# Seven block products for eight in the V and Q projections of a gated linear-attention and Mish kernel

## The chip, the cores and the metric

The kernel runs on one core of a Trainium2 chip. A core has five engines with instruction queues of their own: TensorE (PE, matrix products; PEld is its weight load), VectorE (DVE), ScalarE (ACT), GpSimd (POOL) and SyncE (SP, which here only issues DMAs). An engine takes its instructions in order; semaphores make one wait for another. The metric is the device time of one execution in microseconds (us), the median of several runs. Lower is better.

## What is computed

With S = 2048 rows, width D = 512, 32 heads of 16 columns, and a hidden width of 1376:

```python
g = sigmoid((x * gate_w).sum(-1, keepdims=True))
q, k, v = split(x @ wqkv)                       # each S x 512, 32 heads of 16
pq, pk = per head: q @ w_phi, k @ w_phi
phi = concat(softmax(p), softmax(-p))           # 32 features a head, for pq and for pk
kv, z = phi_k^T v, sum over rows of phi_k       # over all 2048 rows
a = (phi_q kv / (phi_q z + 1e-6)) @ wo
b = mish(x @ w1 + b1) @ w2
return g * a + (1 - g) * b
```

## The kernel before

Every product in fp32r is made of three: each operand is split into a high part (a copy to fp32r, on ACT) and a low part (the rest, a subtraction), and high x high, high x low and low x high are added in PSUM. `w_phi` is multiplied into the weights of K and Q at the start ("fuse").

**Phase A** runs over eight row chunks c = 0..7 of 256 rows, two tiles t of 128 rows each. PE computes K, V and Q of both tiles, each 12 matmuls of 128x128 by 128x512 (`proj`: four k tiles, three products each). For K the features follow: `mx`, `mn`, `d0`, `d1` on DVE (row maxima and differences, from PSUM), `E` on ACT (exp), `S`, `rS`, `ml` on DVE (sum, reciprocal, multiply). `z` on POOL adds E to `zacc`, an SBUF tile. V is copied from PSUM by ACT (`ve`); Q is copied (`qe`) and stored to a DRAM buffer `pqd` (`st`). The product of E and V, `kv`, is 64 small matmuls a chunk into one PSUM bank, issued for several chunks at once. Meanwhile ACT (`xh`) and POOL (`xl`) split the next chunk's x, and `wh`, `wl` split the weights w1 and w2 of phase B, a piece of 1024 columns at a time, all 44 KB a partition of w2 in phase A.

At the end of phase A, `zt zf zs zl` reduce `zacc` over partitions and broadcast it back (`zb`); `km` masks kv.

**Phase B** runs over four blocks of 512 rows. For the hidden slices i = 0..10 of 128 columns PE computes `up` (12 matmuls), ACT the Mish (`mi`) and the high part (`hi`), POOL the low part (`lo`), and PE `dn` (12 matmuls, four row tiles, accumulated over i in four PSUM banks). In between, for each of four row tiles, the features of Q are computed on DVE and ACT (`lq mx mn d0 d1 E S T rS D m de rd sc es tr`), stored to DRAM and read back in another order (`ed`, then `mv` into `eT`), multiplied by kv (`nu`), split (`oh` on ACT, `ol` on DVE), multiplied by wo (`wo`), and joined with the dense branch (`ag`, `fi`), which also stores the output. `XH`, `XL` split x for the next block.

The order is written out by hand: strings of step names (`FIRST`, `MID`, `BLOCK0` and so on) are run one by one, each step appends its instructions to its engine's queue, and `keep_in_program_order` keeps them so. A suffix names another chunk or block: `'` the one before, `"` the one before that, `+` the next. So a step's place in the string fixes its place in each engine's queue, SP's too, where a DMA that waits holds up all behind it. Tiles come from pools with a fixed number of buffers a tag; an allocation waits until an earlier tile of the tag is free. In PSUM, tag `a` has three banks, `dn` four and `kv` one.

Of the kernel before, what the change touches and what calls it, by code (L numbers as in the profile page):

```python
# [32 lines left out]
WARM = 10  # L33

# [11 lines left out]
THREE = MID + """ kv" kv' kv """  # L46
SIXTH = """
    k0 xh mx0 mn0 d00 d10 xl ldx k1 wh0 E0 wl0 ldw0 mx1 mn1 d01 d11 v0 wh1 E1 S0 rS0 ml0 z0 ve0 v1 wl1 ldw1 lq0+
    S1 rS1 ml1 z1 ve1 q0 qe0 st0 q1 qe1 st1 mx0+ mn0+ kv" kv' kv
"""  # L50
NEXT = """
    lq1+ d00+ d10+ k0 xh mx0 mn0 d00 d10 xl ldx k1 wh0 E0 wl0 ldw0 E0+ mx1 mn1 d01 d11 wh1 E1 S0 rS0 ml0 z0 v0 ve0 wl1 ldw1
    S1 rS1 ml1 z1 v1 ve1 q0 mx1+ mn1+ d01+ d11+ qe0 st0 q1 qe1 st1 E1+
"""
LAST = """
    lq2+ k0 mx0 mn0 d00 d10 k1 ldw0 E0 XH0 mx1 mn1 d01 d11 wx E1 v0 S0 rS0 ml0 z0 ve0 XH1 S1 rS1 ml1 z1 XL0
    v1 ve1 mx2+ mn2+ XL1 q0 qe0 st0 q1 qe1 st1 zt zf zs S0+ zl kv' kv rS0+ km
"""

BLOCK0 = """
    up0 lq3 mi0 gr hi0 lo0 ldo0 ldo1 S1 rS1 up1 up2 mi1 hi1 lo1 wh0 wl0 d02 d12 T0 D0 m0 de0 rd0 sc0 es0 tr0 mi2 hi2 up3 dn0 hc lo2
    mi3 hi3 lo3 T1 D1 m1 de1 rd1 sc1 es1 tr1 mv0 lq0+ lq1+ mx3 mn3 d03 d13 WH0 dn1
    up4 mi4 hi4 lo4 WH1 WL0 dn2 E2 S2 T2 rS2 D2 m2 de2 rd2 sc2 es2 tr2 up5 mi5 hi5 lo5 WL1 dn3 E3 ge gg up6 mi6 hi6 lo6 dn4
    up7 mi7 hi7 lo7 dn5 S3 T3 rS3 D3 m3 de3 rd3 sc3 es3 tr3 mv1 up8 mi8 hi8 lo8 dn6
    mx0+ mn0+ d00+ d10+ mx1+ mn1+ d01+ d11+ lq2+ lq3+ up9 mi9 hi9 lo9 dn7 E0+ E1+ S0+ T0+ LX0 rS0+ D0+ m0+ de0+ rd0+ sc0+
    up10 mi10 hi10 lo10 dn8 dn9 cd nu0 nu1 oh0 ol0 es0+ tr0+ XH0+ XL0+ S1+ T1+ rS1+ LX1 df0 df1 wo0 ag0 wo1 oh1 ol1 ag1 D1+ fi0
    m1+ de1+ rd1+ sc1+ df2 df3 wo2 ag2 fi1 XH1+ XL1+ es1+ fi2 wo3 ag3 fi3 tr1+ mv0+
"""  # L70
BLOCK1 = """
    up0 mi0 hi0 lo0 gr mx2 mn2 d02 d12 mx3 mn3 d03 d13 up1 mi1 hi1 lo1 lq0+ lq1+ E2 E3 hc S2 T2 rS2 D2 m2 de2 rd2 sc2 es2 tr2
    up2 mi2 hi2 lo2 dn0 S3 T3 rS3 D3 m3 de3 rd3 sc3 es3 tr3 mv1 up3 mi3 hi3 lo3 dn1 up4 mi4 hi4 lo4 dn2
    mx0+ mn0+ d00+ d10+ mx1+ mn1+ d01+ d11+ lq2+ lq3+ up5 mi5 hi5 lo5 dn3 E0+ E1+ ge gg
    S0+ T0+ rS0+ D0+ m0+ de0+ rd0+ sc0+ es0+ tr0+ up6 mi6 hi6 lo6 dn4 up7 mi7 hi7 lo7 dn5 cd nu0 nu1 oh0 ol0 S1+ T1+ rS1+ D1+ LX0 LX1
    m1+ de1+ rd1+ sc1+ es1+ dn6 wo0 ag0 wo1 ag1 oh1 ol1 tr1+ mv0+ dn7 up8 mi8 hi8 lo8 mx2+ mn2+ d02+ d12+ mx3+ mn3+ d03+ d13+
    wo2 ag2 up9 mi9 hi9 lo9 dn8 E2+ E3+ up10 mi10 hi10 lo10 wo3 ag3 XH0+ XL0+ XH1+ XL1+ dn9 df0 fi0 df1 fi1 df2 fi2 df3 fi3
"""
BLOCK = """
    up0 mi0 hi0 lo0 gr lq0+ lq1+ S2 T2 rS2 D2 m2 de2 rd2 sc2 es2 tr2 up1 mi1 hi1 lo1 hc up2 mi2 hi2 lo2 dn0  # L80
    S3 T3 rS3 D3 m3 de3 rd3 sc3 es3 tr3 mv1 up3 mi3 hi3 lo3 dn1 up4 mi4 hi4 lo4 dn2
    mx0+ mn0+ d00+ d10+ mx1+ mn1+ d01+ d11+ lq2+ lq3+ up5 mi5 hi5 lo5 dn3 E0+ E1+ ge gg
    S0+ T0+ rS0+ D0+ m0+ de0+ rd0+ sc0+ up6 mi6 hi6 lo6 dn4 cd nu0 nu1 oh0 ol0 es0+ tr0+ S1+ T1+ rS1+ D1+ LX0 LX1 m1+ de1+ rd1+ sc1+
    es1+ dn5 wo0 ag0 wo1 ag1 oh1 ol1 tr1+ mv0+ dn6 up7 mi7 hi7 lo7 wo2 ag2 mx2+ mn2+ d02+ d12+ mx3+ mn3+ d03+ d13+
    up8 mi8 hi8 lo8 dn7 E2+ E3+ up9 mi9 hi9 lo9 wo3 ag3 up10 mi10 hi10 lo10 dn8 XH0+ XL0+ XH1+ XL1+ dn9 df0 fi0 df1 fi1 df2 fi2 df3 fi3
"""
# [3 lines left out]
def tile_gated_mix(ctx: ExitStack, tc: tile.TileContext, xT, wv, wkT, wqT, bd, w1a, w1b, b1, w2a, w2b, wo, out):  # L90
# [159 lines left out]
    def feat_ops(key, t, src, d):  # L250
# [7 lines left out]
        def dd(a):  # L258
            if "E" not in d:
                pair = key, t // 2  # L260
                if key == ("A", NCH - 1):
                    d["E"] = k4("E", "oh")
                else:
                    if pair not in Ep:
                        e = T([P, NFB * 512], F32, "w2b", 2, "E")[:, :2048] if key in THIRD else k8("E", "E", F32)[:, :]
                        Ep[pair] = e.rearrange("p (t x) -> p t x", t=2)
                    d["E"] = Ep[pair][:, t % 2, :]
            E = hv(d["E"][:, a * 512 : (a + 1) * 512])
            if a == 0:
                pin(V.tensor_sub(E, hv(src()), d["mx"][:, :, None].to_broadcast([P, H, DH])))  # L270
            else:
                pin(V.tensor_sub(E, d["mn"][:, :, None].to_broadcast([P, H, DH]), hv(src())))  # L272
# [15 lines left out]

    def a_ops(c):
        key = ("A", c)  # L290
        P_ = psA[c] = {}
        for t in range(2):
# [37 lines left out]
            at(key, f"z{t}", lambda d=d: pin(G_.tensor_add(zacc, zacc, d["E"])))  # L330
# [14 lines left out]
        at(key, "kv", kv)  # L345
        if c + 1 < NCH:
# [48 lines left out]
    def w2_tile(f, x):  # L395
        n_, f = ("w2a", f) if f < NFA else ("w2b", f - NFA)
        return W[n_][0][x][:, f * 512 : (f + 1) * 512]

    w2x = {}

    def w2_ops(key):
        def wx():
            h, l = w2_tile(NFA - 1, 0), w2_tile(NFA - 1, 1)
            w2x.update(a=h, b=const.tile([P, 512], F32R, name="w2x"), c=l)
            for dst, o, src, i, n in (("b", 0, h, 0, GROW), ("a", GROW, l, 32, 32), ("b", GROW, l, 0, 32)) + tuple(("c", o, l, 64, 32) for o in (0, 32, 96)):
                pin(Sy.dma_start(f32(w2x[dst][o : o + n, :]), f32(src[i : i + n, :])))

        at(key, "wx", wx)  # L410

# [100 lines left out]
    def b_ops(b):  # L512
# [83 lines left out]
        at(key, "gr", gr)  # L596
        at(key, "ge", ge)
# [294 lines left out]
```

## Time and profile before

| | |
|---|---|
| runs | 444.24, 444.59, 444.80 us; median 444.59 us |
| span of the profiled execution, first to last instruction | 442.5 us; median of the runs less this span: 2.1 us |
| PE / DVE / ACT / POOL busy | 437.8 / 313.2 / 201.4 / 159.6 us |
| DMA | 49.64 MB, mean 112 GB/s |

The profile is of one execution. It comes without a whole time of its own beside the span; so the span, plus the 2.1 us by which the median of the runs exceeds it, stands for that execution's time below. Busy time is the union of an engine's instructions. A chain of waits follows the work back from the last instruction. A row of a group gives line, engine, operation, output<-input, shapes and count, then total busy us and mean ns, then the idle time ahead of them and what ended it. A row of a timeline gives start and duration in us.

### The profile page before, as it was taken

To read this page: it belongs to the slowest core of one execution; us is meant where nothing else is said; L and a number is where in the kernel's file an instruction comes from. 1 tells how busy PE (TensorE), PEld (TensorE's weight loads), DVE (VectorE), ACT (ScalarE), POOL (GpSimd) and SP (SyncE) were. 2 spreads that over 40 slices of the span, in tenths; PEclk is the share of its full clock that TensorE was granted. 3 is DMA by queue.
4 is the path that set the end of the run, shared out by engine and by line. 5 is a ranking of instruction groups with operands and counts; after the bars stand their busy time and mean duration, and the time that the engine had idled before them with its cause. 6 is when DMAs were issued, how large, how long until landed. Compare 5 with 4: busy or idle time off the path is not lost.

```text
span 442.5 us, 7179 instructions
## 1 busy us (share of the span) xinstructions
PE 437.8 (99%) x2874; PEld 359.9 (81%) x2874; DVE 313.2 (71%) x420; ACT 201.4 (46%) x286; POOL 159.6 (36%) x100
## 2 busy tenths in 40 slices
PE   8999999999999999999999999999999999999996
PEld 7888888888888888887888878888878888887885
DVE  3987739559699999999999898279679329601103
ACT  3644523533345455736376533646352645341330
POOL 3078694785662453621024120215310222411121
PEclk9999999999999999999999999999999999999999
DMA  7721631524403136425362533222605302310002
GB/s 265 283 96 48 191 120 50 188 86 133 167 29 116 49 84 209 142 101 168 128 205 96 159 124 120 75 96 95 191 0 192 94 2 96 134 57 1 0 0 96
DMA packets 29001, 49.64 MB, mean 112 GB/s; under 512 B 6308, under 2 KB 15012, under 8 KB 28968
## 3 DMA queue, kind: packets, MB, share of 16 engines
q1 hardware_dynamic: 28648, 48.79, 32.9%
q8 instruction: 22, 0.36, 0.3%
q10 hardware_dynamic: 288, 0.39, 0.3%
q14 instruction: 11, 0.09, 0.1%
q0 software_dynamic: 32, 0.01, 0.0%
HBM read 31.73 MB, written 16.79 MB: 110 GB/s over the span
## 4 chain that ended last, share of the span: by engine, by line
PE 98%; DMA 1%; SPq 0%; DVE 0%; issue 0%
PE proj L101 30%; PE up L101 27%; PE down L101 27%; PE wo L101 10%; PE kvp L101 2%; PE num L101 2%; DMA wT<-in_wkT_dram 1%; PE fuse L101 1%; PE rest L101 0%; DVE io L709 0%; SPq L157 0%; SPq L149 0%
## 5 line engine op out<-in xcount | busy, mean ns | idle before, releaser
L543 POOL TENSOR_TENSOR l<-act,h 128x512 fp32r<-128x512 f32 (+1 forms) x44 | 62.6, 1425 | 215.5 <-ACT h L121 192.7
L121 ACT ACTIVATE act<-up,b1s 128x512 f32<-128x512 f32 x44 | 30.3, 688 | 83.1 <-PE up L101 81.0
L330 POOL TENSOR_TENSOR zacc<-zacc,E 128x1024 f32<-128x1024 f32 x16 | 39.7, 2479 | 39.9 <-DVE E L287 31.4
L121 ACT ACTIVATE E<-E 128x1024 f32<-128x1024 f32 x32 | 33.5, 1060 | 36.0 <-DVE E L272 35.9
L287 DVE TENSOR_TENSOR E<-E,Sm 128x1024 f32<-128x1024 f32 x32 | 45.1, 1409 | 1.0
L101 PE MATMUL wo<-woh,ohl 128*128 128x512 f32 x128 | 41.2, 389 | 0.0
L276 DVE TENSOR_REDUCE Sm<-E 128x64 f32<-128x1024 f32 x32 | 38.5, 1204 | 0.0
L101 PE MATMUL down<-w2ah,h 128*128 128x512 f32 x96 | 37.6, 392 | 0.0
L101 PE MATMUL down<-w2al,h 128*128 128x512 f32 x80 | 31.2, 390 | 0.0
L101 PE MATMUL down<-w2ah,l 128*128 128x512 f32 x80 | 31.1, 389 | 0.0
L121 ACT ACTIVATE h<-act 128x512 fp32r<-128x512 f32 (+2 forms) x48 | 30.3, 632 | 1.6
L101 PE MATMUL down<-w2bh,h 128*128 128x512 f32 x78 | 30.6, 392 | 0.0
L101 PE MATMUL down<-w2bl,h 128*128 128x512 f32 x78 | 30.4, 389 | 0.0
L101 PE MATMUL down<-w2bh,l 128*128 128x512 f32 x78 | 30.4, 389 | 0.0
L431 DVE TENSOR_TENSOR xbl<-xraw,xbh 128x1024 fp32r<-128x1024 f32 x8 | 10.9, 1378 | 27.1 <-ACT xbh L121 27.1
L256 DVE TENSOR_REDUCE mx<-proj 128x32 f32<-128x512 f32 x16 | 11.0, 689 | 25.5 <-PE proj L101 25.5
L101 PEld LDWEIGHTS wo<-woh,ohl 128*128 128x128 f32 x128 | 24.0, 188 | 5.0
L121 ACT ACTIVATE io<-wo,g_sb 128x512 f32<-128x512 f32 x16 | 11.0, 690 | 36.0 <-PE wo L101 34.7
L121 ACT ACT_TABLE_LOAD x19 | 24.4, 1283 | 3.5 <-PE up L101 3.2
L101 PE MATMUL up<-xbh,w1ah 128*128 128x512 f32 x96 | 25.8, 390 | 0.0
L101 PE MATMUL up<-xbh,w1al 128*128 128x512 f32 x96 | 25.7, 389 | 0.0
L101 PE MATMUL up<-xbl,w1ah 128*128 128x512 f32 x96 | 25.7, 389 | 0.0
(125 smaller groups left out, 978.3 us busy)
## 6 DMA issues: line engine op xcount, KB each, us to landing
ed<-E SPq DMA_DIRECT2D x16, 512.0 KB, 2.9
eT<-ed SPq DMA_DIRECT2D x64, 128.0 KB, 3.2
xraw<-in_xT_dram SPq DMA_DIRECT2D x15, 512.0 KB, 4.3
pqd<-qs SPq DMA_DIRECT2D x16, 256.0 KB, 2.1
pq<-pqd SPq DMA_DIRECT2D x16, 256.0 KB, 3.8
out_dram<-io SPq DMA_DIRECT2D x15, 256.0 KB, 2.0
raw<-in_w1a_dram SPq DMA_DIRECT2D x3, 512.0 KB, 4.6
raw<-in_w2a_dram SPq DMA_DIRECT2D x3, 512.0 KB, 3.7
```

Of the source, the lines that this page charges most:

```text
L101: return pin(nc.tensor.matmul(*a, **k))
L121: return pin(A_.activation(out_, in_, fn, **k))
L256: pin(V.tensor_reduce(d[name], hv(src()), axis=AX.X, op=op))
L276: pin(V.tensor_reduce(d["S"], hv(d["E"][:, :]), axis=AX.X, op=ALU.add))
L287: pin(eng.tensor_mul(hv(d["E"][:, :]), hv(d["E"][:, :]), d["S"][:, :, None].to_broadcast([P, 2 * H, DH])))
L330: at(key, f"z{t}", lambda d=d: pin(G_.tensor_add(zacc, zacc, d["E"])))
L431: pin(V.tensor_sub(xb[b][1][:, :, sl], kt(raw[h], SC), f32(xb[b][0][:, :, sl])))
L543: pin(G_.tensor_sub(U[i]["l"][:n, :], U[i]["a"][:n, :], f32(U[i]["h"][:n, :])))
```

## The change

**V and Q of chunks 2 to 7.** Let x of a chunk be cut into four blocks (m, n) of 128 rows by 256 columns, and the weights of V and Q, side by side, into blocks of 256 by 512. The eight block products (each six matmuls: two k tiles, three products) become seven, p1 to p7, in Strassen's scheme. Four of them take sums of x blocks, made in place by POOL (`su`, four additions of 128x256), then split into the tile `sx` by ACT (`sh`) and POOL (`sl`). Four of them take sums of weight blocks, tw1 to tw4, made once in chunks 0 and 1 by DVE (`tA`, `tB`, `tC`), ACT (`tH`) and POOL (`tL`). p1, p6, p7 and p4 accumulate into one PSUM bank, which is read between them: `c1` after p1 (ACT), `c6` after p6 (ACT), `a7` after p7 (DVE), `e4` after p4 (ACT). p5 and p3 share a second bank (`c5` on ACT between them, `a3` on DVE behind), p2 has a third (`a2` on DVE). p4 of a chunk stands behind the next chunk's first K product. PE gets 42 matmuls where it had 48 in each of six chunks.

**E.** The sum over chunks goes to two DRAM tiles `za`: chunk 0 stores its two E, chunks 1 to 6 add theirs by accumulating DMAs issued on POOL's queue; in chunk 6 `zm` adds the second DRAM tile to the first, then the last E is added, and `zr` loads the sum into `zacc`. Chunk 7 is added by POOL as before. The accumulating DMAs on one tile wait for each other.

**w2.** The room that held w2 in phase A holds five buffers of 8 KB a partition (tag `w2`): first the raw sums of weights, tw1 to tw4 and `sx`, then five pairs of w2's slices, which are loaded (`lg`) and split (`gh` on ACT, `gl` on POOL) at the end of chunk 7 and in block 0.

**Order.** The strings are new. kv runs in chunks 2, 4 and 6 for the two chunks before, in chunk 7 for 6 and 7. up0 and up1 of a block move into the end of what stands before it, between dn and wo. The table load for Mish is issued at `pm`, ahead of its use.

```diff
-    k0 xh mx0 mn0 d00 d10 xl ldx k1 wh0 E0 wl0 ldw0 mx1 mn1 d01 d11 v0 wh1 E1 S0 rS0 ml0 z0 ve0 v1 wl1 ldw1
-    S1 rS1 ml1 z1 ve1 q0 qe0 st0 q1 qe1 st1
...
+def chunk(even, b="", c="", d="", e="", x="xh xl su+"):
+    kv, first, then, last = ("kv\" kv'", "S0 rS0 ml0 z0", "mx1 mn1 d01 d11", "c6 E1") if even else ("", "mx1 mn1 d01 d11", "S0 rS0 ml0 z0", "E1 c6")
+    return f"""
+    k0 p4' sh e4' mx0 mn0 d00 d10 {kv} k1 E0 sl {x} ldx {first} p1 c1 p5 c5 wh0 {then} {b} wl0 ldw0 ldw1 p6 {last} wh1 wl1
+    {c} p3 a3 st0 S1 rS1 {d} p7 a7 st1 ml1 z1 p2 a2 {e}
+    """
+CHUNKS = (
+    SECOND, chunk(1), chunk(0), chunk(1), chunk(0, b="lx", e="wx"), chunk(1, b="zm", e="LX0+"),
+    """
+    k0 p4' sh e4' mx0 mn0 d00 d10 kv' k1 E0 sl LX1 zr' XH0 mx1 mn1 d01 d11 p1 c1 p5 c5 E1 XL0 S0 rS0 ml0 lg0* p6 c6 lq0* lg1* XH1 XL1 z0
+    p3 a3 st0 p7 p2 gh0* a7 st1 lq1* lq2* a2 S1 rS1 ml1 z1 up0* mx0* mn0* p4 e4 gr* pm up1* mi0* d00* d10* lq3*
+    kv mx1* mn1* d01* d11* lg2* zt zf zs zl km lg3*
+    """,
+)
...
+BLOCK = """
+    S0 T0 hi0 lo0 gl rS0 D0 m0 de0 rd0 sc0 mi1 hi1 lo1 hc es0 tr0 mx2 mn2 d02 d12 up2 mi2 hi2 lo2 dn0
+    mx3 mn3 d03 d13 S1 T1 rS1 D1 up3 mi3 hi3 lo3 dn1 m1 de1 rd1 sc1 es1 tr1 mv0 E2 E3 ge pm up4 mi4 hi4 lo4 dn2
+    S2 T2 rS2 D2 m2 de2 rd2 sc2 es2 tr2 gg up5 mi5 hi5 lo5 dn3 lq0+ lq1+ up6 mi6 hi6 lo6 dn4 up7 mi7 hi7 lo7 dn5
+    up8 mi8 hi8 lo8 nu0 oh0 ol0 S3 T3 rS3 D3 m3 de3 rd3 sc3 es3 tr3 mv1 dn6 LX0 LX1 wo0 ag0 wo1 ag1
 """
+TAIL2 = """
+    up9 mi9 hi9 lo9 dn7 cd up10 mi10 hi10 lo10 nu1 dn8 oh1 ol1 dn9 wo2 ag2 wo3 ag3 df0 fi0 df1 fi1 df2 fi2 df3 fi3
+"""
...
+        def su(n):
+            r = kt(rawx[c], SC)
+            a, b = {1: ((1, 1), (1, 0)), 3: ((1, 0), (0, 0)), 2: ((0, 0), (1, 1)), 4: ((0, 1), (0, 0))}[n]
+            (o,), (i,) = quarter([r], *a), quarter([r], *b)
+            pin(G_.tensor_add(o, o, i))
+        def product(ps, a, b, start=False):
+            n = 0
+            for x, w in ((0, 0), (0, 1), (1, 0)):
+                for k in range(2):
+                    mm(ps, a[x][:, k, :], b[x * 0 + w][:, k, :], start=(start and n == 0), stop=(n == 5), skip_group_check=True)
+                    n += 1
+        def c6():
+            P_["qs", 0] = k2("qs", "pq")
+            act(P_["qs", 0], d["a"])
+        def a7():
+            pin(V.scalar_tensor_tensor(P_["qs", 1], d["a"], -1.0, P_["qs", 1], op0=ALU.mult, op1=ALU.subtract))
...
-            at(key, f"z{t}", lambda d=d: pin(G_.tensor_add(zacc, zacc, d["E"])))
+            def z_(t=t, d=d):
+                if c == NCH - 1:
+                    pin(G_.tensor_add(zacc, zacc, d["E"]))
+                elif c == 0:
+                    pin(Sy.dma_start(za[t], d["E"]))
+                else:
+                    pin(G_.dma_start(za[t if c < NCH - 2 else 0], d["E"], accum_op=ALU.add))
+        if c == NCH - 2:
+            at(key, "zm", lambda: pin(G_.dma_start(za[0], za[1], accum_op=ALU.add)))
+            at(key, "zr", lambda: pin(Sy.dma_start(zacc, za[0])))
...
+            def gh(g=g):
+                w2g[g] = T([P, 2048], F32R, "w2", 5, f"w2g{g}")
+                act(w2g[g][:, :1024], w2g["raw", g])
```

More of the change, by code (lines that the diff above doesn't have):

```diff
@@ L50 @@
[L50 to L57, printed above, removed]
+    v0 mx0 mn0 d00 d10 mx1 mn1 d01 d11 fq ve0 E0 fh0 fh1 fl0 fl1 fh2 fh3 fl2 fl3 tA0 tA1 E1 xh xl ldx v1 ve1
@@ L58 @@
 """
 BLOCK0 = """
[L63 to L67, printed above, removed]
@@ L78 @@
-"""
[L79 to L85, printed above, removed]
```

217 lines of the change are left out of this document (161 added, 56 removed).

## The prediction

> **What bounds the kernel now.** I read the page first: its engine rows, the granted clock and the chain by engine.
>
> ```profile
> span 442.5 us, 7179 instructions
> PE 437.8 (99%) x2874; PEld 359.9 (81%) x2874; DVE 313.2 (71%) x420; ACT 201.4 (46%) x286; POOL 159.6 (36%) x100
> PEclk9999999999999999999999999999999999999999
> PE 98%; DMA 1%; SPq 0%; DVE 0%; issue 0%
> ```
>
> PE is busy 437.8 of 442.5 us at the full clock, and 98% of the chain that ended last is PE's. But pipelined matmuls cover each other, so a busy PE could still be a PE whose matmuls stand apart. So next the waits of PE alone, and the chain in order of time:
>
> ```profile
> PE warm L101 <- DVE ones L171: 1.1, 1, 1.1
> PE fuse L101 <- DMA wT<-in_wkT_dram: 0.2, 1, 0.2
> ```
>
> ```profile
> 62.56 49.18 PE proj L101 x216
> 111.75 2.82 PE kvp L101 x192
> 221.98 8.16 PE up L101 x36
> ```
>
> PE waits 1.3 us in all, both times at the start. 216 projection matmuls of chunks 3 to 5 take 49.18 us, 0.2277 us each, and 36 of `up` take 8.16 us, 0.2267 us each: the same pace in both phases. So PE's instruction stream is the time, and a matmul left out anywhere is worth 0.227 us, as long as no other engine becomes late. Whether one does is the question. DVE's share by stage (two windows: chunk 5, then block 0 with what surrounds it):
>
> ```profile
> core 0: us, PE busy (x) PEld busy (x) DVE busy (x) ACT busy (x) POOL busy (x), PEclk, DMA share, GB/s
> 95.30:111.70 16.40, 16.40 (x77) 13.32 (x75) 12.63 (x16) 6.39 (x9) 11.81 (x7) 1.00 0.43 145
> 147.50:220.00 72.50, 72.50 (x496) 59.40 (x491) 70.18 (x95) 39.30 (x54) 23.83 (x15) 1.00 0.40 129
> ```
>
> In a chunk DVE has 12.63 of 16.40 us and POOL 11.81; in block 0 DVE has 70.18 of 72.50, and still PE never waited.
>
> **The change part by part.** The rows for the sum:
>
> ```profile
> L121 ACT ACTIVATE E<-E 128x1024 f32<-128x1024 f32 x32 | 33.5, 1060 | 36.0 <-DVE E L272 35.9
> L121 ACT ACTIVATE qs<-proj 128x512 f32<-128x512 f32 x16 | 9.6, 599 | 33.6 <-PE proj L101 33.6
> L121 ACT ACTIVATE xh<-xraw 128x512 fp32r<-128x512 f32 x15 | 8.7, 628 | 0.0
> L121 ACT ACTIVATE w1ah<-raw 128x1024 fp32r<-128x1024 f32 x3 | 3.1, 1048 | 0.0
> L714 DVE SCALAR_TENSOR_TENSOR io<-down,og_sb,io 128x512 f32<-128x512 f32 x15 | 10.7, 747 | 2.5 <-PE down L101 2.5
> L256 DVE TENSOR_REDUCE mx<-proj 128x32 f32<-128x512 f32 x16 | 11.0, 689 | 25.5 <-PE proj L101 25.5
> L276 DVE TENSOR_REDUCE Sm<-E 128x64 f32<-128x1024 f32 x32 | 38.5, 1204 | 0.0
> L287 DVE TENSOR_TENSOR E<-E,Sm 128x1024 f32<-128x1024 f32 x32 | 45.1, 1409 | 1.0
> L248 POOL TENSOR_TENSOR xl<-xraw,xh 128x512 fp32r<-128x512 f32 x14 | 18.7, 1358 | 17.9 <-ACT xh L121 17.9
> L330 POOL TENSOR_TENSOR zacc<-zacc,E 128x1024 f32<-128x1024 f32 x16 | 39.7, 2479 | 39.9 <-DVE E L287 31.4 <-ACT v L121 8.5
> L385 POOL TENSOR_TENSOR w1al<-raw,w1ah 128x1024 fp32r<-128x1024 f32 x3 | 8.2, 2735 | 0.0
> L186 POOL DMA_DIRECT2D b1s<-in_b_dram x1 | 0.7, 676 | 0.0
> ```
>
> *Removed from PE.* Six matmuls in each of six chunks: 36 x 0.227 = **8.2 us**. All other PE work has the same count, only in another order.
>
> *Added to DVE.* `a2`, `a3`, `a7` a chunk, nearest to the `io` row: 3 x 0.75 = 2.2 us, so 12.6 + 2.2 = 14.9 us. PE's chunk is now 66 x 0.227 = 15.0 us, in an even chunk plus two kv (192 small matmuls took 2.82, so 64 take 0.94): 16.9. DVE has 93% of the pair of chunks. That fits, but it leaves no room for waits in DVE's queue. I place them in an even chunk, T its start: k0 ends at 2.7, p4' at 4.1, both kv at 6.0. `d00` needs the E buffer of two chunks before, which kv frees at 5.0. DVE then runs d00, d10, S, rS, ml, the second tile's four, a3 (p3 ends at 14.1), S, rS, a7, ml, a2, and is done 3 to 4 us into the next chunk, whose K arrives at 2.9. The one release that PE needs, a7 before p4', comes at 17.4 to 17.9 against 19.6. Covered, with 1.7 us to spare; price otherwise, the lateness once a chunk.
>
> *ACT in chunks 3 and 5.* Here I find a wait. ACT's queue is c5, wh0, E1, c6, and p7 adds onto the bank that c6 reads. p5 ends at 9.5 (k0, p4', k1, p1, p5: 42 matmuls). The hand-over from PE to ACT, and how far ACT's instructions overlap:
>
> ```profile
> 78.94 1.07 PE L101 MATMUL proj<-wkh,xh 128*128 128x512 f32 x4
> 79.19 0.60 ACT L121 ACTIVATE qs<-proj 128x512 f32<-128x512 f32 x1 [1.81 <-PE proj L101]
> 103.42 1.06 ACT L121 ACTIVATE E<-E 128x1024 f32<-128x1024 f32 x1 [1.65 <-DVE E L272]
> 104.38 0.58 ACT L121 ACTIVATE v<-proj 128x512 f32<-128x512 f32 x1
> ```
>
> Q's matmuls end at 78.94 and its copy starts at 79.19: 0.25 us. An exp starts at 103.42, lasts 1.06, and the next starts at 104.38: 0.1 overlaps. So c6 ends at 9.53 + 0.25 + 0.60 + 1.05 + 1.06 + 0.60 - 3 x 0.1 = 12.8, and with a hand-over of 0.15 p7 starts at 12.95 where PE is ready at 12.25 (p6 and p3 behind p5): 0.7 us, twice, **1.4 us**. In even chunks c6 stands ahead of E1, and c4's second weight piece behind it, so nothing is late there. Other short hand-overs (p6 behind c1, which stands behind an exp and two `xh`, spare 0.3 us): between 0 and 6 x 0.5; I take **0.3**, since the chain gives them spare.
>
> *E by accumulating DMAs, and the end of phase A.* Twelve additions of 2.48 us leave POOL; eleven additions by DMA and `zm` come, and POOL waits for the one before on the same tile. A chunk apart that is free. In chunk 6 it is not: POOL's queue is z0, zm (waits until z0's data have landed), wl0, z1 (waits for zm), and then chunk 7's `sl`, which p5 of chunk 7 needs, and behind `sl` the load LX1 of block 0's x. No accumulating DMA is in the trace. The nearest:
>
> ```profile
> ed<-E SPq DMA_DIRECT2D x16, 512.0 KB, 2.9
> xraw<-in_xT_dram SPq DMA_DIRECT2D x15, 512.0 KB, 4.3
> b1s<-in_b_dram POOLq DMA_DIRECT2D x1, 5.5 KB, 4.6
> ```
>
> A store of the same E lands after 2.9 us; a load of that size and a store one behind the other would be 4.3 + 2.9 = 7.2; POOL's own queue took 4.6 for 5.5 KB. With L for the time from issue to landing, in chunk 6: d10 ends at 6.4, E0 at 7.7, xh at 8.8, two xl at 1.36 end at 11.1, four `su` (half of xl each at least, 0.7 x 4) at 13.9; z0 lands at 13.9 + L, zm at 13.9 + 2L, z1 is issued (0.7) and `sl` runs (2.5): it ends at 17.1 + 2L. p5's fifth matmul, the first that needs it, is due 16.9 + 10.0 = 26.9 after the chunk's start. So PE waits 2(L - 4.9) us. L = 2.9 gives none, 7.2 gives 4.6; I take 5.7, between the row of POOL's queue and the sum of load and store: **1.6 us**. LX1, XH1 and XL1 (4.3 + 1.05 + 2.4) move with it and reach up0 in time within 0.2.
>
> [...]
>
> *Weight sums and w2.* POOL's four `tL` (4 x 2.7) and ACT's `tH` fall in chunks 0 and 1, in place of w1's first pieces; they are due at p5 of chunk 2, some 10 us later. DVE gets 4 x 0.75 and 2 x 1.2 us there: it had 4.5 us free a chunk. In block 0 the five pairs of w2 cost ACT 5 x 1.05 and POOL 10 x 1.36 us, due one pair every two steps of up and dn (10.9 us), against 4.1 us of POOL's time for a pair and its two lo: covered. Cost 0.
>
> *Phase B.* up1 of the next block waits for `ol1`, and dn0 for `lo0`, which by the same hand-overs come within 0.1 us of due time. DVE's row tiles take (first and last instruction of one, then of a slower one, ten each):
>
> ```profile
> 188.24 1.21 DVE L276 TENSOR_REDUCE Sm<-E 128x64 f32<-128x1024 f32 x1
> 194.59 1.25 DVE L626 STREAM_TRANSPOSE E<-E 128x1024 f32<-128x1024 f32 x1
> 177.41 1.21 DVE L276 TENSOR_REDUCE Sm<-E 128x64 f32<-128x1024 f32 x1
> 185.52 1.25 DVE L626 STREAM_TRANSPOSE E<-E 128x1024 f32<-128x1024 f32 x1
> DMA to landing us min/median/max: 2.5/3.2/4.4
> L649 SPq DMA_DIRECT2D eT<-ed x64: 303/432/1033, 174.2 to 387.5; - x64
> ```
>
> 7.6 us or 9.4 us. In block 3 `nu1` follows up10, 18.2 us after nu0's start. In between DVE does `ol0` (done 2.5 us after nu0's start), tile 3 (7.6 to 9.4), the store (2.9), four issues (0.43 each) and a landing (3.2): 17.9 to 19.7. So nu1 waits 0 to 1.5 us; I take **0.7**. nu0 of blocks 1 to 3 by the same steps (two row tiles, two sets of mx to d1 at 3.0) is ready at 32 to 35 against 34.5 us after the block's first up2; I take 0.
>
> *Sum.* -8.2 + 1.4 + 0.3 + 1.6 + 0.7 = **-4.2 us**: span 438.3, and with the 2.1 us around it **440.4 us**.
>
> **The rivals.** A measurement of this kernel can tell about 0.2%, 0.9 us, from no change.
>
> *All covered* (17%): L below 4.9 and E1 early enough, so that only the 36 matmuls count: 444.6 - 8.2, with 0.5 us of short waits 436.9. For it: PE found cover for everything so far. Against: c6's place behind wh0 and E1.
>
> *The accumulating DMA is slow* (13%). Everything else as forecast gives -5.8; it turns at 2(L - 4.9) = 5.8, L = 7.8 us, and at L = 9 the time is 444.6 - 5.8 + 8.2 = 447.0, slower. For it: an accumulate reads, adds and writes, and zm does it from DRAM to DRAM. Against: the DMA engines are busy only 43% in a chunk.
>
> *DVE becomes the bound at nu0* (8%). If each of blocks 1 to 3 has tiles of 9.4 us and more, nu0 waits 1.5 us three times and nu1 1.5: 440.4 + 5.3 = 445.7. For it: block 0's 70.18 of 72.50. Against: DVE has less to do in blocks 1 to 3.
>
> *POOL's DMAs are held by DVE* (8%).
>
> ```profile
> 105.14 1.22 DVE L287 TENSOR_TENSOR E<-E,Sm 128x1024 f32<-128x1024 f32 x1
> 108.11 1.90 DVE L287 TENSOR_TENSOR E<-E,Sm 128x1024 f32<-128x1024 f32 x1
> 106.53 2.39 POOL L330 TENSOR_TENSOR zacc<-zacc,E 128x1024 f32<-128x1024 f32 x1 [3.34 <-DVE E L287]
> ```
>
> The multiply takes 1.22 us alone, 1.90 when it starts beside POOL's addition: one holds the other up. If each of zm and z1 is held for one such multiply, up to 1.9 us, the chain is 3.8 us longer: 444.2, no change. Against: in chunk 6 only `ml` has two SBUF inputs, and zm's issue falls beside operations from PSUM.
>
> [...]
>
> **How the numbers follow.** Forecast 54%, the rivals 17, 13, 8 and 8. Faster by over 0.2%: the first two and a point of the smaller forms of the others, 0.72; within 0.2%: mostly the held DMAs, 0.07; slower 0.21. The likeliest case's own range is 437.5 to 443.5 (L from 4.9 to 7.2, nu1 from 0 to 1.5). The whole range, 436.6 to 446.3, takes in full cover below and DVE at nu0 above, and leaves out most of the slow DMA.
>
> **What would show it.** Right: 36 matmuls fewer, the same 0.227 us; PE waits for ACT's `qs` copy before p7 in chunks 3 and 5 only; one wait for `sx` in chunk 7, twice what zm and z0 take beyond 4.9 us. Wrong: waits of PE in every chunk (DVE or ACT the bound), a wait for `eT` in each block, or an accumulating DMA over 7.8 us.

## The result, and the profile after

| | before | changed |
|---|---|---|
| runs | 444.24 to 444.80 us, median 444.55 | 449.32 to 450.80 us, median 450.52 |
| profiled execution, span | 442.5 us | 449.1 us |
| ratio | | 1.0129, 95% interval 1.0114 to 1.0143 |

The change makes the kernel 6.0 us slower; 440.4 was forecast. The page of the changed kernel, its engine row, granted clock and chain by engine:

```profile
span 449.1 us, 7206 instructions
PE 437.3 (97%) x2838; PEld 352.4 (78%) x2838; DVE 337.7 (75%) x443; ACT 208.2 (46%) x294; POOL 186.8 (42%) x138
PEclk9999999999998999999999999999999999999999
PE 63%; DVE 23%; DMA 6%; POOL 3%; issue 2%; ACT 2%; SPq 1%; DVEq 0%; POOLq 0%
```

The 36 matmuls are gone (2838 for 2874), yet PE is as long busy as before (437.3 for 437.8), one slice shows a lower clock, and PE's share of the chain fell from 98% to 63%. The waits of PE, which before were 1.3 us in all:

```profile
PE proj L102 <- POOL sx L351: 3.6, 1, 3.6
PE kvp L102 <- DVE E L285: 1.5, 1, 1.5
PE warm L102 <- DVE ones L172: 1.1, 1, 1.1
PE proj L102 <- ACT v L122: 0.6, 1, 0.6
PE num L102 <- DMA pq<-pqd: 0.5, 1, 0.5
PE proj L102 <- ACT qs L122: 0.3, 1, 0.3
PE fuse L102 <- DMA wT<-in_wkT_dram: 0.2, 1, 0.2
```

That is 6.5 us of new waits. It does not add up: -8.2 + 6.5 = -1.7, where the span grew by 6.6. So I took the start of every matmul from both traces and compared each stretch with 0.2267 us a large matmul (128x128 by 128x512). The missing 8.3 us have three causes.

**The clock.** PE, its matmuls and its granted clock in four stretches around chunk 7's wait (start:end, length, PE busy, clock, DMA):

```profile
134.20:137.65 3.45, 3.21 (x15) 1.00 0.62 122
137.65:141.06 3.41, 0.00 (x1) 1.00 0.65 78
141.06:144.47 3.41, 3.41 (x8) 0.50 0.92 252
144.47:147.90 3.43, 3.43 (x16) 1.00 0.90 336
```

After the idle stretch the clock is 0.50 for 3.41 us: 8 matmuls there instead of 15, 1.6 to 1.8 us that count as busy. The wait of 3.6 us cost 5.6. Not every run paid that: three, the profiled one among them, had a mean granted clock of 0.995 or 0.996, but the run of 449.32 us had 0.999 (half the clock for 3.41 of 449 us is 0.004 of the mean).

**Changes of matmul shape.** The chain of the changed kernel, in block 1, and of the kernel before, in block 1:

```profile
266.07 1.02 PE num L102 x32
267.09 2.94 PE down L102 x12
```

```profile
259.59 1.89 PE num L101 x64
261.48 2.95 PE down L101 x12
```

Twelve large matmuls take 2.72 us, but 2.94 behind the small ones of num, kv or cd: 0.22 us for each return to large ones. And two groups of 32 take 2.04 us where one of 64 took 1.89. The changed order has num in eight groups for four, kv in five for three, and cd apart from num in three blocks: nine returns more (2.0) and 0.87 us in the groups, **2.9 us**.

**Short hand-overs**, too short for the view of waits, and restarts: behind a stall the second matmul starts some 0.34 us after the first instead of 0.227 (so behind the stalls that end at 73.53, 103.75 and 181.04 us). They are the rest.

| against the kernel before | us |
|---|---|
| 36 matmuls | -8.2 |
| chunk 7, p5 for the split `sl`, and the half clock | +5.6 |
| kv of chunk 1 in chunk 2, for DVE (1.75), and a pause in the kv of chunk 7 (0.3) | +2.1 |
| p7 for c6 in chunk 3 (0.65), p6 for c1 in chunk 5 (1.03), with restarts | +1.7 |
| the second num of block 0 | +1.1 |
| changes of matmul shape, by the counts above | +2.9 |
| hand-overs: up1 and dn0 of three blocks 0.8, two in block 0 0.6 | +1.4 |
| sum | +6.6 |

The pause of 0.3 us in chunk 7 is not DVE's: the trace puts the weight load there behind ScalarE's `v`, and the pause is as long (0.32 us) in the run below that leaves DVE's multiply out.

Two readings stand behind this table. First the multiply `ml` in phase A (20 to 152 us), after and before:

```profile
L285 DVE TENSOR_TENSOR E<-E,Sm 128x1024 f32<-128x1024 f32 x16 | 37.8, 2360 | 0.3
```

```profile
L287 DVE TENSOR_TENSOR E<-E,Sm 128x1024 f32<-128x1024 f32 x16 | 25.5, 1595 | 0.6
```

The same 16 instructions take 12.3 us more. The timeline of the changed kernel around chunk 5 shows why (start, length):

```profile
91.96 2.70 POOL L532 TENSOR_TENSOR w1al<-raw,w1ah 128x1024 fp32r<-128x1024 f32 x1
94.34 2.66 POOL L532 TENSOR_TENSOR w1bl<-raw,w1bh 128x1024 fp32r<-128x1024 f32 x1
...
94.15 3.94 DVE L285 TENSOR_TENSOR E<-E,Sm 128x1024 f32<-128x1024 f32 x1
98.01 0.68 DVE L406 TENSOR_TENSOR v<-proj,v 128x512 f32<-128x512 f32 x1
...
103.75 1.65 PE L102 MATMUL proj<-tw,sx 128*128 128x512 f32 x6 [0.58 <-ACT v L122]
```

The multiply, 1.2 us alone, stands until POOL's second subtraction ends at 97.0; so `a2`, the next chunk's four DVE steps, its exp, ScalarE's `xh` and c1 are late, and PE's p6 waits. Second, POOL's queue in chunk 6:

```profile
121.46 4.07 POOL L343 TENSOR_TENSOR xraw<-xraw 128x256 f32<-128x256 f32 x4
125.46 0.86 POOL L467 DMA_DIRECT2D za<-E  x1
131.68 0.85 POOL L471 DMA_DIRECT2D za<-za  x1 [5.35 <-DMA za<-E]
137.52 0.89 POOL L467 DMA_DIRECT2D za<-E  x1 [3.67 <-ACT v L122]
138.12 2.88 POOL L351 TENSOR_TENSOR sx<-xraw,sx 128x1024 fp32r<-128x1024 f32 x1
```

z0 is issued at 125.46, zm 6.2 us later, z1 5.8 us after that, and then comes the split that PE has waited for since 137.3. This is the forecast's chain.

### The profile page after: what moved, and what is told of

The parts are those of the page before. It is cut to its first block, busy times and chain, and to the rows that moved or that the text cites. A ratio compares the mean times of both kernels' runs of the same rounds, so it can differ in the third digit from the quotient of the medians.

```text
span 449.1 us, 7206 instructions
## 1 busy us (share of the span) xinstructions
PE 437.3 (97%) x2838; PEld 352.4 (78%) x2838; DVE 337.7 (75%) x443; ACT 208.2 (46%) x294; POOL 186.8 (42%) x138
## 4 chain that ended last, share of the span: by engine, by line
PE 63%; DVE 23%; DMA 6%; POOL 3%; issue 2%; ACT 2%; SPq 1%; DVEq 0%; POOLq 0%
PE down L102 20%; PE up L102 20%; PE proj L102 12%; PE wo L102 8%; DVE E L285 4%; DVE Sm L274 3%; DVE E L268 2%; DVE E L270 2%; PE num L102 2%; DMA raw<-in_wv_dram 1%; DMA za<-E 1%; DVE T L788 1%; DVE mx L258 1%; DVE mn L258 1%; DMA za<-za 1%
## 5 line engine op out<-in xcount | busy, mean ns | idle before, releaser
L102 PE MATMUL down<-w2g,h 128*128 128x512 f32 x316 | 98.2, 392 | 0.0
L102 PEld LDWEIGHTS down<-w2g,h 128*128 128x128 f32 x316 | 58.8, 188 | 14.7 <-issue 1.6
L102 PE MATMUL down<-w2g,l 128*128 128x512 f32 x158 | 61.6, 390 | 0.1
L285 DVE TENSOR_TENSOR E<-E,Sm 128x1024 f32<-128x1024 f32 x32 | 58.3, 1823 | 0.9
L102 PEld LDWEIGHTS down<-w2g,l 128*128 128x128 f32 x158 | 29.6, 188 | 6.7 <-POOL l L717 0.5
L102 PE MATMUL proj<-tw,sx 128*128 128x512 f32 x108 | 28.8, 411 | 4.6 <-POOL sx L351 3.6
L891 DVE SCALAR_TENSOR_TENSOR io<-down,og_sb,io 128x512 f32<-128x512 f32 x15 | 11.0, 748 | 25.0 <-ACT io L122 23.8
L102 PEld LDWEIGHTS proj<-tw,sx 128*128 128x128 f32 x108 | 21.0, 198 | 10.4 <-POOL sx L351 4.1
L250 POOL TENSOR_TENSOR xl<-xraw,xh 128x512 fp32r<-128x512 f32 x14 | 19.0, 1402 | 21.9 <-ACT xh L122 21.9
L102 PE MATMUL wo<-wol,ohl 128*128 128x512 f32 x64 | 24.9, 389 | 0.0
```

The lines of the kernel that those rows point to most:

```text
L102: return pin(nc.tensor.matmul(*a, **k))
L250: pin(eng.tensor_sub(xs[c][1][j], kt(rawx[c], SC)[:, 2 * j : 2 * j + 2, :], f32(xs[c][0][j])))
L285: pin(eng.tensor_mul(hv(d["E"][:, :]), hv(d["E"][:, :]), d["S"][:, :, None].to_broadcast([P, 2 * H, DH])))
L891: pin(V.scalar_tensor_tensor(io[t], dn[t], og_sb[:, i : i + 1], io[t], op0=ALU.mult, op1=ALU.add))
```

## The experiments

Runs of the kernel before that stood beside them had medians of 444.5 to 444.7 us.

**Are the 36 matmuls worth anything?** p2 twice:

```diff
-            product(d["c"], xq(0, 1), B((wvh, wvl), 1), True)
+            for _ in range(2):
+                product(d["c"], xq(0, 1), B((wvh, wvl), 1), True)
```

> The changed kernel, with p2 done twice in each of chunks 2 to 7 (its first pass is overwritten), so that PE has the 36 matmuls again. Theory A: 8.2 us more work, of which the waits take back some: p6 behind c1 (0.7), the second kv (0.3), 1.4 of the wait for the split in chunk 7, and with that shorter wait the half clock (1.6): +4.2 us, 454.7 us. Theory B (PE is the bound in every chunk and the waits stay): +8.2 us, 458.7 us. Theory C (DVE or GpSimd bounds the chunks, the 36 matmuls were never worth anything): below 452 us.

Measured: 458.61 us (456.86 to 460.1), ratio 1.0315 (1.0278 to 1.0353). With the work of the kernel before put back it is 8.1 us slower than the changed kernel and 14.1 slower than the kernel before. The runs scatter by 3 us, and the clock has a part in it: the two at a granted clock of 1.0 took 456.9 and 457.2 us, 7.5 to 7.9 above the changed kernel's run at 0.999. So the matmuls bring about what was forecast, and all else in the change costs some 14 us. That is nearer to theory B: the wait for `sl` fell only from 3.6 to 2.4 us, and num now waited 1.6.

**Changes of shape alone**, in the kernel before:

```diff
-    ... dn8 dn9 cd nu0 nu1 oh0 ol0
+    ... cd dn8 nu0 dn9 nu1 oh0 ol0
(and likewise in blocks 1 to 3)
```

> The kernel before, with nothing but the places of small matmuls on PE changed in phase B: cd, nu0 and nu1 stood behind one another in each block and now stand apart, with 12 to 24 large matmuls between them: eight more changes between small and large matmuls, the same instructions. Theory A (each return to 128x128 matmuls costs 0.22 us, each group of num 0.15 us): 0.59 us a block, +2.4 us, 447.0 us, with no wait in PE's table. Theory B (a change costs nothing, the difference in the changed kernel is from waits): 444.6 us.

Measured: 447.05 us, ratio 1.0056 (1.0044 to 1.0068), +2.4 us as worked out. PE's table of waits has no new row. From its chain:

```profile
325.30 1.02 PE num L101 x32
326.32 2.94 PE down L101 x12
```

The same instructions in another order, and eight more changes cost 2.4 us, 0.3 each. That a change of shape has this price is shown; the 2.9 us of the changed kernel are that price times its own nine.

**The chain of accumulating DMAs, moved later** (the late sum):

```diff
-    chunk(1, b="zm", e="LX0+"),            ... E0 sl LX1 zr' XH0 ...
+    chunk(1, e="LX0+") without z1,         ... E0 sl zm' z1' LX1 XH0 ... lg1* zr' XH1 ...
```

> The changed kernel, with only the last additions of E moved: the merge of the two DRAM tiles and chunk 6's second addition are issued by GpSimd behind chunk 7's split of the summed x instead of ahead of it, and the load of the sum stands later in SyncE's queue. Theory A (the two accumulating DMAs hold GpSimd, the split is late, PE idles 3.6 us, and the idle then halves PE's clock for 3.4 us): the wait and the half clock both go, 5.2 us, 445.3 us. Theory B (the clock fell for another reason): only the wait goes, 446.8 us. Theory C (GpSimd or the z sum is late at the next place, up0 or nu0): 448 us or more.

Measured: 449.99 us, ratio 1.0125 (1.0110 to 1.0140): -0.5 us, less than the runs scatter. In the profiled run the wait for `sl` and the half clock went, and as much time was lost elsewhere, theory C; two of the four runs still had a granted clock of 0.996. Its waits and POOL's timeline:

```profile
PE down L102 <- POOL l L717: 3.7, 2, 3.1
PE kvp L102 <- DVE E L285: 1.5, 1, 1.5
PE kvp L102 <- DVE v L406: 0.9, 1, 0.9
```

```profile
132.28 0.85 POOL L471 DMA_DIRECT2D za<-za  x1 [1.70 <-DMA za<-E]
142.60 0.89 POOL L467 DMA_DIRECT2D za<-E  x1 [9.47 <-DMA za<-za]
152.53 4.83 POOL L463 TENSOR_TENSOR zacc<-zacc,E 128x1024 f32<-128x1024 f32 x2 [6.61 <-DMA zacc<-za]
```

POOL waited 9.5 us for the DRAM-to-DRAM addition here, its successor and the load of the sum followed, and POOL reached `lo0` 3.1 us after dn0 was due.

**The same chain, moved earlier** (the early merge):

```diff
-    chunk(1, b="zm", e="LX0+")
+    chunk(1, x="xh xl zm su+", e="LX0+")
```

> The changed kernel, with the merge of the two DRAM tiles moved the other way: issued in chunk 6 ahead of the four sums of x instead of behind the first addition of E, so that one accumulating DMA fewer stands in the chain ahead of chunk 7's split. Theory A (the chain in GpSimd's queue is what is late): the merge at 121.4 us lands at 127.3, the first addition then lands at 133.5, the split ends at 137.0 where p5 is due at 137.3: the wait of 3.6 us and the half clock go, and the end of the z sum comes earlier too, so that nothing takes their place: -5.3 us, 445.2 us. Theory B (whatever is taken away here is lost again at dn0 or nu1 in block 0, since GpSimd or DVE is late as a whole): 448 to 450 us.

Measured: 447.47 us (445.88 to 449.51), ratio 1.0065 (1.0046 to 1.0085): -3.0 us for -5.3. No wait for `sl`, no half clock in the profiled run. What took the place was a wait at chunk 7's kv (0.8 us for DVE's `v`) and lesser ones at up0, dn0 and num: the multiply ahead of that `v`, 1.21 us in the changed kernel, took 2.71 here beside a subtraction of POOL (1.60 us) that now falls beside it. So the chain was a cause, and over half of its price was gained; the rest was lost to lateness behind it.

**The wait filled** with 14 matmuls between the fourth and the fifth of p5 in chunk 7:

```diff
+                    for _ in range(14):
+                        mm(d["c"], xq(0, 0)[0][:, 0, :], wvh[:, 0, :], start=True, stop=True, ...)
```

> The changed kernel, with 14 useless matmuls of 128x128x512 (3.2 us) put in front of the fifth matmul of p5 in chunk 7, where PE waits 3.6 us for the split of the summed x. Theory A (the idle time itself halves the clock): the matmuls fill the wait, the clock stays at 1.0 and the kernel with more work is faster by 1.7 us, 448.8 us. Theory B (the clock fell for another reason): no change, 450.5 us. If the matmuls are not covered by the wait: 453.7 us.

Measured: 452.51 us (450.93 to 454.56): +2.0, theory A's number failed, also in the two runs at a granted clock of 1.0 (450.93 and 451.55). In the profiled run the wait at `sl` was 0.7 us and the clock stayed whole there, as A had it. But

```profile
PE num L103 <- DMA eT<-ed: 2.6, 1, 2.6
```

PE came to block 0's num before DVE's tiles did, waited 2.6 us, and got its half clock there. In the changed kernel's chain DVE stands almost alone from 148.9 to 211.9 us: block 0's row tiles are as long as PE's work beside them.

**The subtractions from POOL to DVE:**

```diff
-   pin(G_.tensor_sub(l[:, cs], raws[n_, cs.start], f32(h[:, cs])))
+   pin(V.tensor_sub(l[:, cs], raws[n_, cs.start], f32(h[:, cs])))
(and the same for tw)
```

> The changed kernel, with the low parts of w1 and of the weight sums subtracted on DVE instead of GpSimd: 11 instructions of about 1.2 us more on DVE, 11 of 2.7 us less on GpSimd. Theory A (DVE's multiply of E, with two inputs in SBUF, stands still while GpSimd subtracts: 3.3 to 4.1 us instead of 1.2): the multiplies fall by some 2 us each, DVE is ahead in spite of the added instructions, and the waits at kv of chunk 2 (1.75), at the kv of chunk 7 (0.3) and at p6 of chunk 5 (0.9) go: -2.9 us, 447.6 us. Theory B (DVE's sum of work is what makes it late): +1.2 us a chunk, the waits grow, 452 us or more.

Measured: 452.85 us, ratio 1.0178 (1.0158 to 1.0198): +2.3. The multiplies fell as theory A said, from a mean of 2.36 us to 1.46, but the added instructions took as much, and DVE's busy time from 20 to 152 us stayed at 116.5 (116.6), with one multiply fewer in that window. The first kv then waited 2.1 us for 1.5, and that brought a half clock of its own.

```profile
L285 DVE TENSOR_TENSOR E<-E,Sm 128x1024 f32<-128x1024 f32 x15 | 22.0, 1464 | 0.3
```

**The subtractions halved**, with the early merge:

```diff
+                for o in range(cs.start, cs.stop, 512):
+                    pin(G_.tensor_sub(l[:, o : o + 512], ...
(and the same for tw and sx)
```

> The kernel with the early merge of the DRAM tiles (447.5 us), with GpSimd's subtractions of 1024 columns (low parts of w1, of the weight sums and of the summed x) made as two of 512 each, the same arithmetic. Theory H (a GpSimd instruction with two SBUF inputs holds DVE's multiply for its whole length, and DVE gets in between two of them): the multiplies that took 2.9 to 4.1 us take 2.6 at most, the wait for kv in chunk 2 falls from 1.5 to 0.3, those for ScalarE and for DVE at p6 and kv of chunk 7 go: 444.5 us. If the next GpSimd instruction gets in ahead of DVE: nothing changes, 447.5 us.

Measured: 448.03 us (445.67 to 451.05), no change against the early merge alone. Theory H held in part. Beside the halved weight sums in chunks 0 and 1, DVE got in between two halves: two multiplies took 2.16 and 2.32 us that had taken 3.22 and 3.42, and the wait at chunk 2's kv fell from 1.5 to 0.6 us. Around chunk 5 it did not:

```profile
91.46 2.83 POOL L535 TENSOR_TENSOR w1al<-raw,w1ah 128x512 fp32r<-128x512 f32 x2
93.96 2.81 POOL L535 TENSOR_TENSOR w1bl<-raw,w1bh 128x512 fp32r<-128x512 f32 x2
...
93.64 4.21 DVE L285 TENSOR_TENSOR E<-E,Sm 128x1024 f32<-128x1024 f32 x1
```

The multiply stood behind three half instructions in a row. And in the profiled run, one of 451.05 us, `sl` was waited for again (3.0 us), with a half clock of 6.8 us behind it.

**DVE's multiply left out**, with the early merge:

```diff
-            at(key, f"ml{t}", lambda d=d: scale_by(d, V))
+            at(key, f"ml{t}", lambda d=d: scale_by(d, V) if c in (0, NCH - 1) else None)
```

> The kernel with the early merge of the DRAM tiles (447.5 us), with DVE's multiply of E by the reciprocal sums left out in chunks 1 to 6: E goes on unscaled; some 25 us less of DVE's time, all else is there. Theory D (DVE is late in the chunks because this multiply stands behind GpSimd's subtractions): the waits for DVE and, behind it, for ScalarE go (kv of chunk 2, p6 of chunk 5, p7 of chunk 3, kv of chunk 7: 4.7 us with their restarts), 442.8 us. Theory P (GpSimd is the one that is late, DVE only waits for it): the waits stay, 446.5 us or more.

Measured: 444.89 us, ratio 1.0016 (0.9996 to 1.0036): -2.6 us for -4.7. E goes on unscaled here, so DVE has less work of its own too. All waits for DVE in chunks 2 to 7 are gone, and so is p6 for c1; the longest that are left, besides the first matmul's, are

```profile
PE proj L102 <- ACT qs L122: 0.7, 2, 0.4
PE up L102 <- POOL xbl L605: 0.4, 1, 0.4
```

p7 waits for c6 in chunks 3 and 5, which is the forecast's own place: with DVE in time, it shows in both chunks.

**The subtractions on neither engine**, with the early merge. ScalarE makes plain copies in their place, so the subtraction is left out:

```diff
-    pin(G_.tensor_sub(l[:, cs], raws[n_, cs.start], f32(h[:, cs])))
+    act(l[:, cs], raws[n_, cs.start])
(and the same for tw)
```

> The kernel with the early merge of the DRAM tiles (447.5 us), with the low parts of w1 and of the weight sums made as plain copies on ScalarE (the subtraction is left out), so that neither GpSimd nor DVE has these 11 instructions of 1024 columns. Theory D (GpSimd's subtractions hold DVE's multiplies): the multiplies that took 2.9 to 4.1 us take 1.2, DVE gains some 15 us over the chunks without losing any, and the waits for DVE and ScalarE go: 443 us. Theory S (ScalarE, with 1.05 us a piece more, becomes late): new waits for ScalarE, 446 us or more. If DVE's own sum of work is what counts (the held multiplies only fill its idle time): 447 us.

Measured: 446.68 us, ratio 1.0060 (1.0043 to 1.0077). Again no wait for DVE, though it keeps all its work: its 16 multiplies from 20 to 152 us took 23.8 us instead of 40.9 with the early merge alone, and its busy time there fell from 122.4 to 107.4. So DVE's waits end when the holding ends, though PE, itself late for ScalarE, left DVE some more time: ScalarE's c6 now stood behind the copies as well (3.3 us of waits in four places), theory S.

**c6 ahead of the exp**, without the other edits. In every chunk the weight pieces `wh0`, `wl0` and their loads move behind p6 as well:

```diff
-    ... c5 wh0 {then} {b} wl0 ldw0 ldw1 p6 E1 c6 wh1 wl1
+    ... c5 {then} {b} p6 c6 E1 wh0 wl0 ldw0 ldw1 wh1 wl1
```

> The changed kernel, with ScalarE's copy c6 ahead of the exp E1 and of the weight pieces in the odd chunks too. Theory A: the wait of p7 in chunk 3 (0.5 and 0.13 for the restart) goes, in chunk 5 the wait is that of p6 for c1 and stays: -0.6 us, 449.9 us. As the prediction had it (both chunks): -1.4 us, 449.1 us. If the exp is then late for DVE: no gain.

Measured: 449.98 us, ratio 1.0110 (1.0090 to 1.0130): -0.5 us. Both waits, of p7 and of p6, left the profile, but the wait for `sl` was 3.8 us, and the half clock behind it lasted 6.8 us instead of 3.4. By time alone this does not tell the theories apart.

**Together.** Four edits with the late sum and the subtractions on DVE:

```diff
(late sum, wl and tw's low parts on V, c6 as above, and)
-    (BLOCK) ... lo8 nu0 oh0 ol0          (TAIL, TAIL2) ... cd up10 ...
+    (BLOCK) ... lo8 nu0 cd oh0 ol0       (TAIL, TAIL2) ... up10 ...
```

> The changed kernel with four edits together: the last additions of E behind chunk 7's split, the low parts of w1 and of the weight sums on DVE, c6 ahead of the exp, and cd beside nu0 in blocks 1 to 3 (three returns fewer, 0.7 us). Theory A adds up: -5.2 - 2.9 - 0.6 - 0.7 = -9.4 us, 441.1 us, below the kernel before (444.6). If the waits are one lateness that moves from place to place: 445 us or more.

Measured: 452.44 us, ratio 1.0178 (1.0160 to 1.0196); the gains did not add up. Two of its parts, the late sum and the subtractions on DVE, gained nothing alone either. Then three edits (early merge, c6 as above, cd beside nu0):

> The changed kernel with the early merge of the DRAM tiles, c6 ahead of the exp in odd chunks, and cd beside nu0 in blocks 1 to 3. Theory A: -5.3 for the chain, -1.6 for the waits at p7 of chunk 3 and p6 of chunk 5 (both were gone in the profile with c6 moved), -0.7 for three changes of matmul shape: 443.0 us. Theory B (lateness of DVE and GpSimd moves on): 446 us or more.

Measured: 446.38 us (444.93 to 447.24), ratio 1.0037 (1.0022 to 1.0051): with the kernel of 446.30 us below, the fastest with all work, 4.1 us below the changed kernel, 1.9 above the kernel before. With kv moved behind k1, and with halved subtractions:

```diff
-    chunk 2: ... kv" kv' k1 ...
+    chunk 2: ... kv" k1 kv' ...
```

> As the one with the three edits, and the kv of chunk 1 issued behind the second K product of chunk 2 instead of ahead of it (one more group of small matmuls, 0.35 us, for the wait of 1.75 us): 441.6 us by theory A, faster than the kernel before. If PE's lead of 1.4 us is lost again behind DVE in chunks 2 to 7: 443 us, no gain over the three edits.

> The three edits (446.4 us: early merge, c6 ahead of the exp, cd beside nu0) with the halved GpSimd subtractions. Theory H: 446.4 less the waits for DVE that were left (kv of chunk 2 1.5, kv of chunk 7 1.1, part of the 1.2 at the split): 443.2 us, faster than the kernel before. Otherwise 446.4 us.

Measured: 447.54 us (ratio 1.0073, 1.0054 to 1.0091) and 446.30 us (1.0045, 1.0028 to 1.0062). In the first, the wait of 1.5 us at kv was gone, and waits of 0.4 to 1.7 us for ScalarE and `sl` took its place. In the second, it was 0.6 us, but `sl` was waited for twice, 2.6 us in all, and a half clock followed. Chunk 7 by eight products:

```diff
-            if c < PLAIN:
+            if c < PLAIN or c == NCH - 1:
(and chunk 7's string with v0 ve0 v1 ve1 q0 qe0 q1 qe1 for p1 to p7)
```

> As the one before, with chunk 7's V and Q by eight products as in the kernel before (six matmuls more, no sums, no split and no wait for it in chunk 7; DVE without three and GpSimd without five instructions there): PE +1.4 us, less the waits that chunks 6 and 7 still have (0.7 to 2 us): 442.5 to 443.5 us. If those waits are already gone with the halves: 444.5 us.

Measured: 449.45 us, ratio 1.0110 (1.0085 to 1.0134). Not what I expected: in the order I wrote for chunk 7, an `up` of block 0 stood behind Q's copy (2.4 us) and ScalarE came late to block 0. It says nothing on the products.

**All named places at once**, the three edits with DVE's multiply left out:

> The kernel with the three edits (early merge, c6 ahead of the exp, cd beside nu0; 446.4 us), with DVE's multiply of E left out in chunks 1 to 6 (E goes on unscaled). If the places found are all there is: the run without the multiply (444.9 us) less the waits of p7 for c6 in chunks 3 and 5 (1.3 with restarts) and less three returns to large matmuls (0.7): 442.9 us, and no wait of PE over 0.5 us in chunks 2 to 6. If another engine is late behind DVE: 444.5 us or more.

Measured: 443.41 us, ratio 0.9973 (0.9961 to 0.9985). PE's waits:

```profile
PE warm L102 <- DVE ones L172: 1.1, 1, 1.1
PE up L102 <- POOL xbl L605: 0.4, 1, 0.4
...
PE down L102 <- POOL l L717: 0.3, 1, 0.3
PE proj L102 <- POOL sx L351: 0.2, 1, 0.2
```

In chunks 2 to 6 nothing waits, and the time is 0.5 us above the sum: of the 2.0 us that c6 and three returns were to bring, 1.5 came, in runs that scatter by 3 us. So these places were rightly named, but they are not all there is. 443.4 us is still 7.0 above what 36 matmuls fewer alone would give (444.6 - 8.2). The returns that are left make some 2.2 of that (2.9 - 0.7, an estimate from the counts); of the rest, the profile shows 2.3 us in short hand-overs of chunk 7 and block 0, and what is left stays open. With DVE's multiply in, no version run here beats the kernel before.

## Why the prediction was wrong, step by step

Three steps failed above all. The work that is only reordered was priced at nothing and lost 2.9 us. DVE was called covered, but its multiplies are held beside POOL (1.75 us at the first kv, 1.03 at p6 of chunk 5). And chunk 7's split was sized at 1.6 us and cost 5.6, with the half clock.

- *36 matmuls, -8.2*: right; 8.1 us in the run that put them back, 7.5 to 7.9 between runs at full clock.
- *p7 behind c6, 1.4*: 0.65 in chunk 3; in chunk 5 it was p6 behind c1, 1.03. That the two add up to nearly 1.4 is luck, since the second is another wait. The step itself was right once DVE was in time: without its multiply, p7 was behind c6 in both chunks, 0.63 us each.
- *Short hand-overs, 0.3*: 1.4.
- *Chunk 7's split, 1.6*: here a term was mis-sized, and not by the part that I doubted. The accumulating DMA was taken as 5.7 us; it is (from issue to landing, median)

```profile
za<-E POOLq DMA_DIRECT2D x12, 512.0 KB, 5.4
za<-za POOLq DMA_DIRECT2D x1, 512.0 KB, 5.3
```

 z0's own took 5.7. What failed is the start of the chain: a sum of 128x256 was costed at half of an `xl` (0.7) and takes 1.0, and a subtraction of w2 (1.6) ahead of chunk 6's own `sl` was not counted, so that z0 was issued 16.0 us into chunk 6, 2.1 later than reckoned. From issue to issue in the chain 6.2 and 5.8 us passed. The wait was 3.6 us. And a wait was priced at its length: the half clock behind it, another 1.7, is in no step. The trace has it: PE 0.00 us busy from 137.65 to 141.06, then 3.41 us at a clock of 0.50.
- *Weight sums, cost 0*: failed, 1.75 at the first kv. "It had 4.5 us free a chunk" reckoned DVE's instructions at their length before. Beside POOL's subtractions for the weight sums the two multiplies of chunk 1 took 3.4 and 3.0 us.
- *DVE, 93% of a pair of chunks, covered*: the share came out (30.8 of 33.1 us busy in chunks 4 and 5), but by luck, and the word covered was wrong. The window behind the 12.63 us holds 16 of DVE's instructions where a chunk has 14 (two chunks of the kernel before, 62.5 to 95.3 us, have 22.9 us). What was counted too much there, the multiplies took: four in 11.0 us, where the windows of before have 1.22 and 1.90 a chunk, 6.2. I had the row in which the multiply takes 1.90 beside POOL's addition and used it only for a rival on POOL's DMAs. The multiplies of 3.9 to 4.2 us go further than that row: DVE waited through two and three of POOL's instructions, though between the halves of the weight sums it got in.
- *nu1, 0.7 in block 3*: nothing there. The second num of block 0 lost 1.1, for which no term stood, by the same chain (DVE's tiles, store, loads). The size is near by luck.
- *"All other PE work has the same count, only in another order"*: the step that I did not see to be one. 2.9 us, at the price that the split run shows. A return to large matmuls is 0.22 us of it.
- *The likeliest case's own range, 437.5 to 443.5*: its bounds (L from 4.9 to 7.2, nu1 from 0 to 1.5) give 438.1 to 444.2. The result is outside both.

The gap between the forecast span of 438.3 us and the profiled one of 449.1 is 10.8 us: 4.0 at chunk 7's split, 2.1 at kv, 2.9 for the shapes, 1.8 for the rest. None of the rivals had this: the slow accumulate needed L over 7.8, and L was 5.4.

What stays open is whether an order exists that keeps all work and DVE in time. DVE was late through the sum of its own work and of the time it is held; either part moved (e.g. the subtractions to DVE) left the sum.

## What to carry to other kernels

An engine at 99% is not the only bound when another stands at 93% in the same stage, and a busy share also counted the time for which instructions were held (the 16 multiplies of phase A stand as 37.8 us of it, 25.5 before): work taken from the first turns into waits that move from place to place, and a cure of one wait must be followed to where it comes back. When small and large matmuls are reordered, count the changes between them, 0.3 us each here. And cost an instruction by who runs beside it, not by its mean: DVE's multiply with two inputs in SBUF, 1.2 us alone, took up to 4.2 beside GpSimd's instructions.

## What the hardware showed that I had not expected

**The clock fell by windows, not by the length of a wait.** In the traces' records of the clock, the full-speed stretches last 136.53 and 303.79 us in the changed kernel and 436.91 in the kernel before: 40, 89 and 128 times the 3.413 us of the half clock between the first two. On that grid, the late-sum kernel's wait of 3.1 us fell across two windows, and the clock held; the four-edit kernel's 2.1 us at kv fell into one window with small matmuls around it, and it fell:

```profile
153.78:157.20 3.42, 1.79 (x8) 1.00 0.69 190
157.20:160.60 3.40, 1.96 (x9) 1.00 0.12 45
```

```profile
47.50:50.90 3.40, 1.33 (x77) 1.00 1.04 180
50.90:54.30 3.40, 3.40 (x9) 0.50 0.86 130
```

In the profiled runs, windows of 3.4 us with 1.63 us of large matmuls (the four-edit kernel from 98.70 us, the kernel with p2 twice from 144.70) or 1.79 (late sum) kept the clock, and those with 0.28 (c6 moved, from 136.30) or 0.00 (the changed kernel, from 137.65) lost it; with small matmuls among them, 1.33 us (four edits) and 1.75 (the wait filled, from 200.40) lost it, and 2.17 (the changed kernel, from 45.48) kept it. So the wait of 3.1 us brought no half clock and the one of 2.1 us brought 3.4 us of it. The runs of the kernel with c6 moved show the price: 447.55 us at a granted clock of 0.999, 448.71 at 0.996, 449.87 to 450.94 at 0.992. The kernels made from the changed one scatter by 1.3 to 5.4 us from run to run, the kernel before by 0.6 to 1.6. The clock is only a part of that: with kv moved behind k1, the runs go from 446.56 to 449.83 us at 0.999 to 1.0. The rest of the scatter stays open.

**An accumulating DMA of 512 KB** landed 5.4 us after its issue from SBUF (median of 12; 5.2 to 7.3) and 5.3 from DRAM. In the late-sum kernel the one from DRAM took 9.8 (issued at 132.28 us; the instruction that waited for it started at 142.60); the reason was not tested. **A tiny DVE instruction was held like a long one**: `den` (128x32, two SBUF inputs) took 0.19 us alone and up to 2.29 beside POOL in block 0 of the changed kernel (from 197.12 to 199.41 us, where a subtraction of POOL ended at 199.36).
